# Indirect writes of routed rows placed step by step, and block 2's rows loaded and transposed later, in a recurrence-plus-experts kernel

## The chip, the cores and the metric

One core of one Trainium2 chip runs the whole kernel; the other cores are idle. The metric is device time in microseconds of one execution, lower is better. The kernel before took 364.48 us in the median of three runs (362.39, 364.92, 364.48).

The engines are called as in the profile: PE (TensorE, the matrix engine; its weight loads are PEld), DVE (VectorE), ACT (ScalarE), POOL (GpSimd) and SP (SyncE, which here only issues transfers). Each engine runs its own list of instructions in order and waits for the others on semaphores.

## The reference, cut to what matters

```python
# r, k, v, w: (4, 8, 768, 48); u: (8, 48)
for t in range(S):                       # a recurrence over 768 steps for each batch and head
    cur = u * k_t (outer) v_t
    y[:, :, t] = r_t @ (state + cur)
    state = w_t * state + k_t (outer) v_t
x = y.transpose(0, 2, 1, 3).reshape(3072, 384)
logits = x @ w_gate + modality_bias[modality_id]       # 8 experts
e_idx = argmax(logits); gate_w = softmax(logits)[e_idx]
for e in range(8):                       # each row goes through one expert only
    out[rows of e] = gate_w * (relu(x @ w1[e]) @ w2[e])   # 384 -> 1024 -> 384
```

## The kernel before

**Two stages.** The first stage (the scan, `att_iter`) goes through 24 units of 128 rows, one iteration `i` of a software pipeline each, and leaves each unit's 128 x 384 result (with its gate weight and row id, 386 columns) in SBUF. The second stage runs the experts over blocks of rows sorted by expert: blocks 0 and 1 have 512 rows, blocks 2 to 4 have 384, block 5 has 512 and block 6 has 416. A block is gathered by a plain load from the DRAM tensor `xs`, in which each row has been put at its sorted place.

**How rows get to their place.** Unit n is written by one indirect DMA on POOL's queue (`scatter(n)`, L692), 128 rows of 1544 bytes; the row numbers stand in column n of `posT`. They come from a count on PE into the PSUM tile `pR` (`route_b`) and one DVE reduction of all units of a part (L573 and L574). Part 0 is units 0 to 9, ranked during the scan; part 1 is units 10 to 23, ranked at the beginning of block 0's second half. `drain(n)` (L858) issues the next n writes that are due. The table `DRAIN` (L64) says after which scan iteration how many are issued: one each after iterations 15 to 20, and four after iteration 21. `LOAD` (L67) says after which iteration blocks 0 and 1 are loaded: 20 and 22. A load of `xs` waits for all writes issued before it, and a write behind a load waits until the load has read. Part 1's 14 writes are issued two at each of the steps 2 to 8 of block 0's down phase (L934).

**A block.** `blk_t` (L723) transposes a block's rows on PE into four PSUM pieces; ACT copies them rounded (`xh`), DVE takes the rest (`xo`). The up phase has 8 steps g of 9 matmuls (`blk_up`, L748), written alternately to two PSUM tiles pS0 and pS1; ACT makes `hh` of it and DVE `hl`, and only then is the PSUM tile free for step g + 2. The down phase goes through the block's groups j of 128 rows with 4 steps of 6 matmuls each (`blk_down`), step number 4j + g; each group is scaled by ACT (`ot`, L800) and written to `out` by an indirect DMA on POOL (L801). During these phases the weights are split into a rounded part and a rest for the next use: `w_split(1, ...)` (the second matrix, ACT cast L272 into `wh1`, DVE L273 into `wl1`) at the up steps 0, 2, 4 and 6, and `w_split(0, ...)` (the first one) in the down phase. For block 0 the first matrix is split at the scan's end with POOL doing the rests, three pieces in iteration 22 and five in iteration 23 (`split_some`, L326). The buffers `wh1` and `wl1` lie where the scan's tiles lay, part 0's rows among them, so their first cast waits until all ten writes of part 0 have read these rows.

**The order.** Everything is in program order, written by hand. What is interleaved with a block stands in a list by block, phase and step (`at(q, "u" or "d", step, ...)`), which `run` calls after that step's matmuls. `pad_rows` (L682) writes 128 zero rows behind each expert's rows, from SP's queue, at block 1's up steps 0 to 3, two each; SP issues them as soon as the counts are known. Block 2's load is issued at block 1's up step 4, and its `blk_t` stands between block 1's up and down phases:

```python
        for g in range(FC):
            blk_up(q, g)
            run(q, "u", g)
        if nxt is not None:
            blk_t(nxt)
        for j in range(nj):
            for g in range(FC // 2):
                blk_down(q, (2 * g, 2 * g + 1), (j,))
```

Of the kernel before, what the change touches and what calls it, by code (L numbers as in the profile page):

```python
# [14 lines left out]
ALU = mybir.AluOpType  # L15
AX = mybir.AxisListType

B, H, S, D = 4, 8, 768, 48
P = 128
NCH = S // P  # L20
NU = B * NCH
NT = B * S
DM = H * D
E, F = 8, 1024
KC = DM // P
FC = F // P
# [12 lines left out]
WB = NWA  # L39
# [15 lines left out]
PART = (10, 14)  # L55
FROM = (0, PART[0])
# [4 lines left out]
NEARLY = 3  # L61
SCATTER = PART[0] + 3
NEAR = 6
DRAIN = {**{SCATTER + 2 + n: 1 for n in range(NEAR)}, NU - 3: PART[0] - NEAR}  # L64
EARLY = 6
NPW = 3
LOAD = (SCATTER + 1 + NEAR, NU - 2)  # L67


@with_exitstack  # L70
def kernel(ctx: ExitStack, tc: tile.TileContext, rkw, vt, wf, cst, mid, wg, bias, w1, w2, out):
    nc = tc.nc
# [25 lines left out]
    def wt(n, tag, sh, bufs=None, dt=F32):  # L98
        T[tag, n] = (pa if tag in PREP else wk if tag in WORK else rt).tile(sh, dt, tag=tag, name=f"{tag}{n}", bufs=bufs)
        return T[tag, n]  # L100

    def pt(n, tag, sh=(P, 512)):
        T[tag, n] = (bp["s"] if tag in ("pS0", "pS1") else ps).tile(list(sh), F32, tag=tag, name=f"{tag}_{n}")
        return T[tag, n]
# [70 lines left out]
    posT = cp.tile([P, NU], I32, name="posT")  # L175
# [109 lines left out]
    def busy(i):  # L285
        return i in DRAIN and i < NU - 3

# [221 lines left out]
    units = lambda c: slice(FROM[c], FROM[c] + PART[c])  # L509
# [4 lines left out]
    def rcol(o, *sh):  # L514
        n = 1
        for d in sh:
            n *= d
        v = T["R"][:, o:o + n]
        return v if len(sh) == 1 else v.rearrange("p (a b) -> p a b", a=sh[0])

    C_RK, C_TAB = NU * E, 2 * NHX * E
# [34 lines left out]
    def route_b(c):  # L556

        n, oh = PART[c], T["oh", c]
        sh, ne = [P, n, E], NE(c)
        pR = T["R"][:, C_RK:C_RK + ne + 2 * E]  # L560

        def add(out, lhsT, rhs, start=False, stop=False):
            nc.tensor.matmul(out=out, lhsT=lhsT, rhs=rhs, start=start, stop=stop, skip_group_check=True)

        add(pR[:, 0:ne], trib, oh.rearrange("p a b -> p (a b)"), True)
        add(pR[:, 0:ne], onesb, ersb[:, None, :].to_broadcast(sh))
        if c:
            add(pR[:, 0:ne + E], onesb, ohs[:, None, :].to_broadcast([P, n + 1, E]))

        for j in range(n):  # L570
            m = n + (c == 0 and j < NEAR)
            add(pR[:, (j + 1) * E:(m + 1) * E], onesb, oh[:, j:j + 1].to_broadcast([P, m - j, E]), stop=j == n - 1)
        po, rk = posT[:, units(c)], rcol(C_RK, n, E)  # L573
        nc.vector.tensor_reduce(out=po, in_=rk, axis=AX.X, op=ALU.min)  # L574
        sm = wt(c, "sm", [P, NMOST, 1], 1)[:, 0:n]
        nc.vector.tensor_reduce(out=sm, in_=ex[:, 0:n], axis=AX.X, op=ALU.add)
        nc.vector.reciprocal(out=T["xp", c][:, :, DM:DM + 1], in_=sm)

    MAGIC = 12582912.0

# [105 lines left out]
    def rows_apart(key, ins):  # L686

        tc.declare_no_dep(ins.ins, group=key, reason="disjoint rows")
        tc.add_to_no_dep_group(key, ins.ins)

    def scatter(n):
        rows_apart("xs", nc.gpsimd.indirect_dma_start(out=xs[:, :], out_offset=bass.IndirectOffsetOnAxis(ap=posT[:, n:n + 1], axis=0),  # L692
                                     in_=T["xb", n], in_offset=None, bounds_check=XROWS - 1, oob_is_err=False))
# [12 lines left out]
    def width(q):  # L706
        return WIDTH[q] if isinstance(q, int) else BT

    def spans(w):
        return [(c, min(c + P, w)) for c in range(0, w, P)]  # L710

    def blk_load(q, at=None):
        at = q if at is None else at
        w = width(q) // P
        rest = width(q) % P
        xl = bp["m"].tile([P, BW // P, XW], F32, tag="xl", name=f"xl{q}", bufs=3)
        r = nc.sync.value_load(tab[0:1, 1, ds(at, 1)], min_val=0, max_val=DUMMY)
        nc.sync.dma_start(out=xl[:, 0:w], in_=xs[ds(r, w * P), :].rearrange("(j p) c -> p j c", p=P))
        if rest:
            nc.sync.dma_start(out=xl[0:rest, w], in_=xs[ds(r + w * P, rest), :])  # L720
        X["xl", q] = xl

    def blk_t(q):  # L723
        xl, w = X["xl", q], width(q)
        xh, xo = (bp["m"].tile([P, KC, BW], F32R, tag=t, name=f"{t}{q}", bufs=1) for t in ("xh", "xo"))
        pk, pu, nj = pt(f"x{q}_0", "pK", (P, 2, 512)), pt(f"x{q}_2", "pU"), w // P
        halves, m = [(0, KC - 1, (pk[:, 0], pk[:, 1])), (KC - 1, KC, (pu, pt(f"x{q}_3", "pX")))], w % P
        for c0, c1, pp in halves:
            for c in range(c0, c1):
                for j in range(nj):  # L730
                    for pb, r in zip(pp, HALVES):
                        o = ((c - c0) * nj + j) * 64
                        nc.tensor.transpose(out=pb[:, o:o + 64], in_=xl[r, j, c * P:(c + 1) * P], identity=ident[r, r])
        o = 64 * nj
        for c in range(KC if m else 0):
            nc.tensor.transpose(out=pu[:, o + c * m:o + (c + 1) * m], in_=xl[0:m, nj, c * P:(c + 1) * P], identity=ident[0:m, 0:m])
        view = lambda t, c0, c1, h: t[:, c0:c1, 0:nj * P].rearrange("p c (j h b) -> p c j h b", h=2, b=64)[:, :, :, h]
        moves = [(lambda t, c0=c0, c1=c1, h=h: view(t, c0, c1, h), pb[:, 0:(c1 - c0) * nj * 64].rearrange("p (c j b) -> p c j b", c=c1 - c0, j=nj))
                 for c0, c1, pp in halves for h, pb in enumerate(pp)]
        if m:  # L740
            moves.append((lambda t: t[:, :, nj * P:w], pu[:, o:o + KC * m].rearrange("p (c b) -> p c b", c=KC)))
        for at, pp in moves:
            nc.scalar.copy(out=at(xh), in_=pp)
        for at, pp in moves:
            nc.vector.tensor_tensor(out=at(xo), in0=pp, in1=at(xh).bitcast(F32), op=ALU.subtract)
        X["x", q] = (xh, xo)
# [109 lines left out]
    pend = []  # L856

    def drain(n):  # L858
        for _ in range(n):
            if pend:  # L860
                scatter(pend.pop(0))

    def hook_b(c):
        route_b(c)
# [2 lines left out]
    for i in range(-2, NU):  # L867
# [19 lines left out]

        drain(DRAIN.get(i, 0))
        if i in LOAD:
            blk_load(LOAD.index(i))  # L890
    assert not pend and not hooks
# [9 lines left out]
    seq = [*range(NQ)]  # L901
# [11 lines left out]
    def at(q, ph, step, *fn):  # L913
        aux.setdefault((q, ph, step), []).extend(fn)
# [5 lines left out]
    part = lambda fn, *a, **k: (lambda: fn(*a, **k))  # L920
    q0, q1 = seq[0:2]
# [8 lines left out]
    at(q0, "u", FC - 1, part(next, ra1), part(next, ra1), part(blk_raw, q1, 1))  # L930
    at(q0, "d", 0, part(route_x, 1))
    at(q0, "d", 1, part(hook_b, 1))
    for g in range(2, 4 * FC // 2):
        at(q0, "d", g, part(drain, 2))  # L934
        if g < 6:
            at(q0, "d", g, part(w_split, 0, g - 2))
        if 5 <= g < 8:
            at(q0, "d", g, part(more_table, 1, 2 - g // 7))
# [4 lines left out]
            at(q, "u", FC - 1, part(blk_raw, nq, 1))  # L943
    for e in range(E):
        at(q1, "u", e // 2, part(pad_rows, e))
    at(q1, "u", 4, part(blk_raw, seq[2], 0), part(blk_load, seq[2]))
    for k, q in enumerate(seq[1:1 + NG // 2]):
        for n, ph, step in ((2 * k, "u", 2), (2 * k + 1, "u", 6)):
            at(q, ph, step, part(guard_load, n))
# [11 lines left out]
    for n, q in enumerate(seq):  # L961
        nxt, nxt2 = (seq[n + d] if n + d < len(seq) else None for d in (1, 2))
        if nxt is None:
            bad, end, endh, rest = (nc.values_load(flg[0:1, i:i + 1], min_val=lo, max_val=hi)  # L964
                                    for i, lo, hi in ((0, 0, P), (1, NQ, HO), (2, HO, NTAB), (3, 0, P + NTAB)))
        nj = len(spans(width(q))) - (nxt is None)
        for g in range(FC):
            blk_up(q, g)
            run(q, "u", g)
        if nxt is not None:  # L970
            blk_t(nxt)
        for j in range(nj):
            for g in range(FC // 2):
                blk_down(q, (2 * g, 2 * g + 1), (j,))
                if nxt is not None and q != q0 and j == 0:
                    w_split(0, g)
                run(q, "d", (FC // 2) * j + g)
            if nxt2 is not None and q != q0:
                if j == 0:
                    blk_raw(nxt2, 0)  # L980
                if j == (2 if q == q1 else 0):
                    blk_load(nxt2)
            if q >= DRAIN_FROM and j == 0:
                nc.gpsimd.drain(fusable=False)  # L984
            if nxt is None and j == 1:
                strip_sum(q, nj)
                blk_out(q, (nj,))
            blk_out(q, (j,))
            if nxt is None and j == 0:
                strip_down(q, nj)  # L990
# [183 lines left out]
```

## Time and profile before

| what | value |
|---|---|
| median of three runs | 364.48 us (362.39 to 364.92) |
| the profiled execution, its own time | 362.38 us |
| its span (first to last instruction) | 360.6 us |
| mean granted PE clock over the span | 0.972 |
| PE busy | 338.0 us, 94% |
| DVE / ACT / POOL busy | 62% / 57% / 43% |
| end of the scan, first expert matmul | 129.4 us |
| block 1's up phase | 166.7 to 195.0 us |

The page shows one profiled execution. Times are us from the span's start. "Idle before" is what an engine waited ahead of an instruction and what ended that wait; "issue" means that nothing in the profile shows what the engine waited for, "remote" likewise for a semaphore whose sender is not seen. A granted clock of 1.00 is 2.4 GHz, 0.50 is 1.2 GHz. Matmul ends are modelled, so neighbouring rows of PE overlap; the distance of their starts is the pace.

### The profile page before, as it was taken

The page shows a single profiled execution, that of the slowest core. Times are in us where ns is not written, and L with a number is a line of the kernel's source. Part 1 is how long each engine was busy: PE and PEld are TensorE (multiplying, and loading weights), DVE is VectorE, ACT ScalarE, POOL GpSimd, SP SyncE. Part 2 cuts the span into 40 slices and gives each one's busy share as a digit, 9 for nine tenths or more (in the row PEclk, how much of TensorE's full clock was granted, in tenths as well). Part 3 has the DMA queues.
Part 4 walks back from the last instruction along what each step waited for, and adds up shares of the span by engine and source line. Part 5 has one row for each costly group of instructions (what it writes and reads, how often), then busy time and mean ns, then how long its engine had stood idle before and what let it go on. Part 6 is the DMA issues. An engine that isn't in the chain of part 4 may idle for free.

```text
span 360.6 us, 10329 instructions
## 1 busy us (share of the span) xinstructions
PE 338.0 (94%) x4064; PEld 306.5 (85%) x4064; DVE 224.4 (62%) x478; ACT 206.2 (57%) x524; POOL 155.1 (43%) x194
## 2 busy tenths in 40 slices
PE   8899999999989799997499999999999999999993
PEld 3688899989889687896278999999999988999973
DVE  6999999999997244880057936946526525814500
ACT  2576687878789373620046835956956934614320
POOL 5889999999982860077410220120120120121013
PEclk9999999999999789999589999999999999999998
DMA  7977887778864320036640430160260442210001
GB/s 229 399 242 227 287 291 267 248 258 259 284 225 135 97 82 0 3 139 249 217 164 3 148 137 2 29 236 0 51 236 2 153 158 89 88 58 29 1 25 56
DMA packets 18910, 52.30 MB, mean 145 GB/s; under 512 B 2405, under 2 KB 10405, under 8 KB 18852
## 3 DMA queue, kind: packets, MB, share of 16 engines
q1 hardware_dynamic: 15748, 42.08, 35.3%
q0 software_dynamic: 3104, 9.47, 7.0%
q8 instruction: 34, 0.56, 0.7%
q14 instruction: 24, 0.20, 0.2%
HBM read 55.43 MB, written 11.88 MB: 187 GB/s over the span
## 4 chain that ended last, share of the span: by engine, by line
issue 52%; PE 11%; POOL 9%; POOLq 2%; DMA 1%; ACT 0%; DVE 0%; ACTq 0%
POOL out L801 6%; PE pY L445 3%; POOL xs L692 2%; PE pS L401 2%; PE pY L434 1%; POOLq L984 1%; PE pR_x L317 1%; PE pR_x L494 1%; PE pU L419 1%; DMA xs<-xp,posT 1%; PE pS_u L756 1%; POOL wl L273 1%; POOLq L801 0%; POOLq L964 0%; POOL xp L549 0%
## 5 line engine op out<-in xcount | busy, mean ns | idle before, releaser
L801 POOL DMA_INDIRECT out<-ot,xl x25 | 26.0, 1039 | 157.8 <-ACT ot L800 156.6
L761 DVE SCALAR_TENSOR_TENSOR hl<-pS_u,hh 128x512 fp32r<-128x512 f32 (+2 forms) x56 | 34.6, 618 | 88.3 <-ACT hh L760 74.8
L756 PE MATMUL pS_u<-xh,wh 128*128 128x512 f32 (+2 forms) x168 | 63.1, 375 | 3.0 <-issue 3.0
L756 PE MATMUL pS_u<-xh,wl 128*128 128x512 f32 (+2 forms) x168 | 62.4, 371 | 2.4 <-issue 2.4
L760 ACT ACTIVATE hh<-pS_u 128x512 fp32r<-128x512 f32 (+2 forms) x56 | 30.3, 541 | 51.7 <-PE pS_u L756 50.3
L273 DVE TENSOR_TENSOR wl<-raw,wh 128x768 fp32r<-128x768 f32 x52 | 48.2, 954 | 3.1 <-ACT wh L272 2.6
L756 PE MATMUL pS_u<-xo,wh 128*128 128x512 f32 (+2 forms) x168 | 44.2, 369 | 1.7 <-issue 1.7
L272 ACT CAST wh<-raw 128x768 fp32r<-128x768 f32 (+1 forms) x60 | 45.1, 800 | 0.0
L756 PEld LDWEIGHTS pS_u<-xh,wh 128*128 128x128 f32 x168 | 32.1, 191 | 9.0 <-issue 5.9
L692 POOL DMA_INDIRECT xs<-xp,posT x24 | 24.9, 1040 | 32.3 <-issue 25.0
L777 PE MATMUL pY_d<-wh,hh 128*128 128x384 f32 x112 | 38.5, 344 | 0.0
L777 PE MATMUL pY_d<-wl,hh 128*128 128x384 f32 x112 | 37.6, 336 | 0.0
L777 PE MATMUL pY_d<-wh,hl 128*128 128x384 f32 x112 | 37.6, 336 | 0.0
L756 PEld LDWEIGHTS pS_u<-xh,wl 128*128 128x128 f32 x168 | 32.1, 191 | 5.8 <-issue 2.8
L756 PEld LDWEIGHTS pS_u<-xo,wh 128*128 128x128 f32 x168 | 31.3, 190 | 5.0 <-issue 1.6
L331 DVE TENSOR_TENSOR_SCAN pX_s<-pw,pX_s 128x268 f32<-128x268 f32 x48 | 34.1, 710 | 1.1 <-POOL pw L278 0.8
L283 POOL TENSOR_TENSOR G<-in 128x512 f32<-128x512 f32 x24 | 31.0, 1293 | 4.6 <-DMA in<-rkw 4.6
L445 PE MATMUL pY<-v,A 128*64 128x48 f32 x768 | 29.0, 225 | 2.9 <-issue 2.9
L342 ACT ACTIVATE dV<-v,dT 128x48 f32<-128x48 f32 x120 | 29.7, 325 | 0.1
L445 PEld LDWEIGHTS pY<-v,A 128*64 128x64 f32 x768 | 26.3, 141 | 4.0 <-issue 3.7
L403 DVE TENSOR_TENSOR A<-pS,cs 128x1024 f32<-128x1024 f32 x24 | 29.2, 1217 | 0.6 <-PE pS L401 0.6
L401 PE MATMUL pS<-R,K 64*128 64x128 f32 x384 | 26.9, 280 | 2.0 <-DVE A L403 1.2
(327 smaller groups left out, 679.9 us busy)
## 6 DMA issues: line engine op xcount, KB each, us to landing
raw<-w SPq DMA_DIRECT2D x24, 768.0 KB
in<-rkw SPq DMA_DIRECT2D x22, 768.0 KB
v<-vt SPq DMA_DIRECT2D x24, 192.0 KB
wg<-wf SPq DMA_DIRECT2D x8, 576.0 KB
raw<-w SPq DMA_DIRECT2D x8, 384.0 KB
xl<-xs SPq DMA_DIRECT2D x3, 772.0 KB
xl<-xs SPq DMA_DIRECT2D x4, 579.0 KB
xs<-zt SPq DMA_DIRECT2D x8, 193.0 KB
```

The costliest lines, as they stand in the source:

```text
L272: nc.scalar.copy(out=wh[k][:, sl], in_=raw[k][:, sl])
L273: (eng or (nc.vector, nc.gpsimd)[k]).tensor_tensor(out=wl[k][:, sl], in0=raw[k][:, sl], in1=wh[k][:, sl].bitcast(F32), op=ALU.subtract)
L283: nc.gpsimd.tensor_tensor(out=G, in0=t[:, 0:512], in1=t[:, 512:1024], op=ALU.mult)
L331: nc.vector.tensor_tensor_scan(out=BE[:, ::step], data0=pp[:, ::step], data1=d1[:, ::step], initial=0.0, op0=ALU.mult, op1=ALU.max)
L401: nc.tensor.matmul(out=pS[:, hh, p], lhsT=K[q, p], rhs=R[q, p], start=True, stop=True)
L445: nc.tensor.matmul(out=pY[q:q + 64, h * D:(h + 1) * D], lhsT=A[:, hh, p, q:q + 64], rhs=v[:, h * D:(h + 1) * D], start=(first(z) and h == ...
L692: rows_apart("xs", nc.gpsimd.indirect_dma_start(out=xs[:, :], out_offset=bass.IndirectOffsetOnAxis(ap=posT[:, n:n + 1], axis=0), in_=T["xb ...
L756: nc.tensor.matmul(out=pp, lhsT=wsrc[0][:, g, c * P:(c + 1) * P], rhs=xsrc[:, c, 0:w], start=(n == 0), stop=(n == 3 * KC - 1))
L760: nc.scalar.activation(out=hh, in_=pp, func=AF.Relu)
L761: nc.vector.scalar_tensor_tensor(out=hl, in0=pp, scalar=0.0, in1=hh.bitcast(F32), op0=ALU.max, op1=ALU.subtract)
L777: nc.tensor.matmul(out=X["y", q, j][0:r1 - r0], lhsT=hsrc[:, r0:r1], rhs=wsrc[1][:, f], start=(f == 0 and n == 0), stop=(f == FC - 1 and n ...
L801: ins = nc.gpsimd.indirect_dma_start(out=out[:, :], out_offset=bass.IndirectOffsetOnAxis(ap=xl[0:m, j, DM + 1:DM + 2].bitcast(I32), axis=0 ...
```

## The change

Three things. The 10 early writes: one each after iterations 15 to 22 and two after iteration 23, instead of one each to 20 and four after 21; block 1's load goes from iteration 22 to 23, behind the last of them. The 14 later writes: at block 0's down steps 2, 3, 4, 8 and 12, at block 1's eight up steps, and at its down step 0, one each; and the DVE reduction that makes a unit's row numbers is no longer made once for all 14 but one column at each write's step, just ahead of it in program order. Block 2: its load goes from block 1's up step 4 to its down step 1, its transposes from ahead of block 1's down phase to ahead of the last of its four groups; one of the PSUM pieces is then `pS1` in place of `pX`.

```diff
-DRAIN = {**{SCATTER + 2 + n: 1 for n in range(NEAR)}, NU - 3: PART[0] - NEAR}
+DRAIN = {**{SCATTER + 2 + n: 1 for n in range(PART[0] - 2)}, NU - 1: 2}
...
-LOAD = (SCATTER + 1 + NEAR, NU - 2)
+LOAD = (SCATTER + 1 + NEAR, NU - 1)
...
-        po, rk = posT[:, units(c)], rcol(C_RK, n, E)
-        nc.vector.tensor_reduce(out=po, in_=rk, axis=AX.X, op=ALU.min)
+        if c == 0:
+            place(0, n)
...
+    def place(n, k):
+        c = int(n >= PART[0])
+        nc.vector.tensor_reduce(out=posT[:, n:n + k], in_=rcol(C_RK + (n - FROM[c]) * E, k, E), axis=AX.X, op=ALU.min)
...
-        halves, m = [(0, KC - 1, (pk[:, 0], pk[:, 1])), (KC - 1, KC, (pu, pt(f"x{q}_3", "pX")))], w % P
+        halves, m = [(0, KC - 1, (pk[:, 0], pk[:, 1])), (KC - 1, KC, (pu, pt(f"x{q}_3", "pS1" if q == WB else "pX")))], w % P
...
-                scatter(pend.pop(0))
+                n = pend.pop(0)
+                if n >= PART[0]:
+                    place(n, 1)
+                scatter(n)
...
+    for q, ph, steps in ((q0, "d", (2, 3, 4, 8, 12)), (q1, "u", range(FC)), (q1, "d", (0,))):
+        for g in steps:
+            at(q, ph, g, part(drain, 1))
     for g in range(2, 4 * FC // 2):
-        at(q0, "d", g, part(drain, 2))
...
-    at(q1, "u", 4, part(blk_raw, seq[2], 0), part(blk_load, seq[2]))
+    at(q1, "u", 4, part(blk_raw, seq[2], 0))
+    at(q1, "d", 1, part(blk_load, seq[2]))
...
-        if nxt is not None:
+        if nxt is not None and q != q1:
             blk_t(nxt)
         for j in range(nj):
+            if q == q1 and j == nj - 1:
+                blk_t(nxt)
```

**Place 1, POOL at the scan's end.** xs<-xp is a write of one unit's rows, dV belongs to the scan, wl is the rest of block 0's first matrix, xp<-tidi fills in the row ids of part 1.

```order
 L354 TENSOR_TENSOR dV_2540<-v_2298,dT_2469 128x192
-L692 DMA xs<-xp_385,posT 29184x386 x4
-L354 TENSOR_TENSOR dV_2652<-v_2411,dT_2589 128x192
+L696 DMA xs<-xp_385,posT 29184x386
+L354 TENSOR_TENSOR dV_2643<-v_2411,dT_2589 128x192
 L273 TENSOR_TENSOR wl_69<-raw_66,wh_68 128x384 x3
-L354 TENSOR_TENSOR dV_2738<-v_2524,dT_2683 128x192
+L696 DMA xs<-xp_385,posT 29184x386
+L354 TENSOR_TENSOR dV_2721<-v_2524,dT_2674 128x192
 L273 TENSOR_TENSOR wl_69<-raw_66,wh_68 128x384 x5
+L696 DMA xs<-xp_385,posT 29184x386 x2
 L549 COPY xp_1423<-tidi 128x14
```

The four writes in a row become one, one and two; the last two now stand behind all eight rests of block 0's first matrix.

**ACT at block 0's first up steps**, the same in both kernels. wh_2864 is `wh1`; the names that begin with DMASW are the semaphores of POOL's writes.

```order
L760 ACTIVATE hh_0_2880<-pS_u_0_2870 128x512 [waits DMAHW3_49,DMAHW2_49,DMAHW5_49,PE_49,Activation_49]
L481 COPY xT_2886<-pX_('x', 0)_2885 128x384 [waits PE_49]
L272 CAST wh_2864<-raw_67 128x768 [waits DMASW4_49,DMASW3_49,DMASW5_49,DMASW2_49,DMASW6_49,DMASW1_49,DMASW7_49,DMASW0_49,DMAHW7_49,Activation_49,Pool_49]
L760 ACTIVATE hh_1_2903<-pS_u_1_2893 128x512 [waits PE_49]
L481 COPY xT_2908<-pX_('x', 1)_2907 128x384 [waits PE_49]
L760 ACTIVATE hh_2_2923<-pS_u_2_2913 128x512 [waits PE_49]
```

Nothing moved here; the cast waits for the writes of place 1, and the second up step's `hh_1` stands behind the cast.

**Place 2, POOL from block 0's down phase on.** Before:

```order
L692 DMA xs<-xp_1423,posT 29184x386 x4
L801 DMA out<-ot_0_3128,xl_2529 3072x384
L692 DMA xs<-xp_1423,posT 29184x386 x8
L801 DMA out<-ot_1_3216,xl_2529 3072x384
L692 DMA xs<-xp_1423,posT 29184x386 x2
L801 DMA out<-ot_2_3252,xl_2529 3072x384
L801 DMA out<-ot_3_3282,xl_2529 3072x384
L801 DMA out<-ot_0_3609,xl_2726 3072x384
```

And in the changed kernel, on the same engine:

```order
L696 DMA xs<-xp_1423,posT 29184x386 x2
L805 DMA out<-ot_0_3123,xl_2529 3072x384
L696 DMA xs<-xp_1423,posT 29184x386
L805 DMA out<-ot_1_3191,xl_2529 3072x384
L696 DMA xs<-xp_1423,posT 29184x386
L805 DMA out<-ot_2_3225,xl_2529 3072x384
L696 DMA xs<-xp_1423,posT 29184x386
L805 DMA out<-ot_3_3259,xl_2529 3072x384
L696 DMA xs<-xp_1423,posT 29184x386 x9
L805 DMA out<-ot_0_3591,xl_2821 3072x384
```

Nine of the 14 writes now stand behind block 0's last output write; each of the nine waits for its own DVE reduction, which stands behind that up step's `hl` on DVE.

**Place 3, PE around block 1's down phase** (xl_3465 and xl_3544 hold block 2's rows). Before, ahead of the first group:

```order
L756 MATMUL pS_u_7_3509<-xo_3029,wh_68 128x512 x3
L733 MATMUL pK_x_0_3527<-cs,xl_3465 128x64 x12
L733 MATMUL pU_x_2_3528<-cs,xl_3465 128x64
L733 MATMUL pX_x_3_3529<-cs,xl_3465 128x64
L733 MATMUL pU_x_2_3528<-cs,xl_3465 128x64
```

Now, between the third group and the fourth:

```order
L781 MATMUL pY_d_2_3656<-wh_2864,hl_7_3514 128x384
L737 MATMUL pK_x_0_3723<-cs,xl_3544 128x64 x12
L737 MATMUL pU_x_2_3724<-cs,xl_3544 128x64
L737 MATMUL pS_x_3_3725<-cs,xl_3544 128x64
L737 MATMUL pU_x_2_3724<-cs,xl_3544 128x64
```

The same 18 transposes moved behind three groups of the down phase.

## Rows read from the trace of the kernel before

**Rows 1.** Busy time of each engine, page part 1.
```profile
PE 338.0 (94%) x4064; PEld 306.5 (85%) x4064; DVE 224.4 (62%) x478; ACT 206.2 (57%) x524; POOL 155.1 (43%) x194
```

**Rows 2.** Stages: from:to, length, busy by engine (instructions), PE clock, DMA share, GB/s.
```profile
122.00:124.50 2.50, 1.74 (x22) 1.27 (x23) 0.00 (x0) 0.06 (x1) 2.48 (x4) 0.50 0.29 110
124.50:129.40 4.90, 4.90 (x90) 4.76 (x90) 2.50 (x5) 3.99 (x12) 2.30 (x4) 0.57 0.54 165
149.20:166.70 17.50, 17.50 (x119) 17.28 (x114) 11.49 (x42) 5.89 (x11) 9.91 (x9) 1.00 0.38 136
166.70:180.00 13.30, 6.39 (x18) 3.59 (x17) 0.00 (x0) 1.11 (x3) 7.86 (x8) 0.74 0.65 224
```

**Rows 3.** Waits, 166 to 183 us: us in total, times, longest.
```profile
ACT ot L800 <- remote: 19.7, 2, 10.1
...
PE pS_u L756 <- issue: 7.1, 9, 1.1
```

**Rows 4.** Timeline of PE, block 1's up phase: start, us, instruction.
```profile
166.73 0.39 PE L756 MATMUL pS_u<-xh,wh 128*128 128x512 f32 x1
...
179.60 1.48 PE L756 MATMUL pS_u<-xo,wh 128*128 128x512 f32 x3
181.32 0.80 PE L756 MATMUL pS_u<-xh,wh 128*128 128x512 f32 x1 [0.24 <-issue]
...
184.42 0.40 PE L756 MATMUL pS_u<-xh,wh 128*128 128x512 f32 x1
...
186.52 0.40 PE L756 MATMUL pS_u<-xh,wh 128*128 128x512 f32 x1
...
195.01 0.59 PE L733 MATMUL pK_x<-cs,xl 64*128 64x64 f32 x12
```

**Rows 5.** Timelines of POOL (two writes) and SP (zero rows), 154 to 172 us.
```profile
154.23 1.79 POOL L692 DMA_INDIRECT xs<-xp,posT  x1 [19.54 <-issue]
...
165.60 0.98 POOL L692 DMA_INDIRECT xs<-xp,posT  x1 [0.30 <-issue]
...
159.25 12.15 SPq L684 DMA_DIRECT2D xs<-zt  x6
```

**Rows 6.** The group of L692, first and last start; PE's longest wait, 84 to 112 us.
```profile
L692 POOL DMA_INDIRECT xs<-xp,posT x24: 968/982/1787, 85.2 to 174.6; - x24
...
PE pY L445 <- issue: 0.7, 1, 0.7
```

**Rows 7.** Timelines of POOL and SP, end of the scan.
```profile
109.08 0.99 POOL L692 DMA_INDIRECT xs<-xp,posT  x1 [0.15 <-issue]
...
117.59 1.00 POOL L692 DMA_INDIRECT xs<-xp,posT  x1 [6.98 <-DMA xl<-xs]
...
128.88 4.91 POOL L273 TENSOR_TENSOR wl<-raw,wh 128x384 fp32r<-128x384 f32 x5 [2.60 <-ACT wh L272]
...
111.98 12.88 SPq L718 DMA_DIRECT2D xl<-xs  x2
```

**Rows 8.** PE's waits, 118 to 124 us.
```profile
PE pY L445 <- issue: 1.6, 4, 0.5
...
PE pR_x L494 <- ACT dT L319: 0.7, 1, 0.7
```

**Rows 9.** Timelines of PE, ACT and DVE at block 0's up phase.
```profile
129.43 0.50 PE L756 MATMUL pS_u<-xh,wh 128*128 128x512 f32 x1
...
137.03 0.51 PE L756 MATMUL pS_u<-xh,wh 128*128 128x512 f32 x1
...
132.74 0.85 ACT L272 CAST wh<-raw 128x768 fp32r<-128x768 f32 x1
...
133.62 1.00 DVE L273 TENSOR_TENSOR wl<-raw,wh 128x768 fp32r<-128x768 f32 x1
134.90 0.69 DVE L761 SCALAR_TENSOR_TENSOR hl<-pS_u,hh 128x512 fp32r<-128x512 f32 x1 [0.28 <-ACT hh L760]
```

**Rows 10.** Timeline of DVE: the reduction that the change cuts up.
```profile
152.72 0.26 DVE L574 TENSOR_REDUCE posT<-pR_x 128x14 int32<-128x112 f32 x1
```

## The prediction

> **What bounds the kernel now.** I read the busy times first: PE is busy for 338.0 of 360.6 us [rows 1], so only time in which PE stands still or runs at the lower clock is to be had. The busy times by stage say where: in the whole second half PE has one hole, block 1's up phase [rows 2]. From 166.7 to 180.0 us it is busy for 6.39 of 13.3 us, at a mean granted clock of 0.74, beside a DMA share of 0.65. The timeline gives the size: from the first up matmul at 166.73 to the transposes at 195.01 are 28.3 us [rows 4]; eight undisturbed steps of 2.10 us (184.42 to 186.52, same rows) are 16.8. So 11.5 us are lost there.
>
> The waits say how. PE waits nine times for "issue", 7.1 us in all, and ACT waits for "remote" for 19.7 us ahead of two evictions [rows 3]. So no engine waits for data that another one is late with; instructions themselves come late, on PE, ACT and SP alike. SP needs 12.15 us for six plain writes of zero rows [rows 5], two us each. At that time POOL issues its indirect writes without a break, one in 1.28 us (0.98 of work and 0.30 of gap), from 154.23 on [rows 5] to the last at 174.6 [rows 6]. The same picture stands, smaller, at the scan's end: four writes in a row from 117.59 on [rows 7], and PE waits four times for "issue" and once for ACT, 2.3 us together [rows 8], then runs at a clock of 0.50 and 0.57, that is mostly at 1.2 GHz, until 129.4 [rows 2]. Against that, six single writes between 85.2 us [rows 6] and 109.08 [rows 7], some 4.8 us apart, leave PE with no wait for "issue" over 0.7 us [rows 6]. I read this as: indirect writes back to back hold up the delivery of instructions, single ones hardly do.
>
> **The early writes (place 1).** What goes: 2.3 us of waits [rows 8]. The low clock behind them covers 7.4 us in which PE is busy for 6.6 [rows 2]; at 2.4 GHz that work would be shorter by a third at most, since small matmuls don't double: 2.4 us. So the first expert matmul, now at 129.43, could come 4.7 us earlier, at 124.7, and the fourth up step, now at 137.03 [rows 9] and 7.6 us behind the first, at 132.3.
>
> What comes: a wait. The last two early writes now stand on POOL behind the five rests of 4.91 us, which begin at 128.88 and wait for ACT's casts [rows 7]. PE's earlier pace brings ACT's casts forward, but by less than 4.7 us, since ACT has its own work ahead of them; I take 3.1 us. Then the rests end at 130.7, the ninth write starts at 130.85 and the tenth at 132.15. How long a write needs to land: the sixth starts at 109.08 and the load that waits for it starts at 111.98 [rows 7], 2.9 us. So the tenth lands at 135.05. For that ACT's first cast into `wh1` waits, and behind the cast on ACT stands `hh_1`, behind the rest on DVE stands `hl_1`, and the fourth up step waits for `hl_1`'s PSUM tile. Cast 0.85, rest 1.00, `hl` 0.69 [rows 9], some 0.1 of semaphores: the fourth step starts at 137.7 instead of 137.03. Before it PE stands still for 5.4 us (132.3 to 137.7), and I expect the clock at 1.2 GHz for the next steps, as behind the hole of block 1. There the three matmuls from 179.60 take 1.72 us to the next start instead of 0.70, and the nine from 181.32 to 184.42 take 3.10 instead of 2.10 [rows 4], 2.0 us together. So the scan's end costs 0.7 + 2.0 = 2.7 us where four writes in a row cost nothing net.
>
> Bounds: if the cast doesn't wait, 4.7 us are won. If PE is no earlier at all, the writes start 3.1 us later, the fourth step comes at 140.8, and with the clock 5.8 us are lost. I take +2.7, since the wait is in the program and only the shift of 3.1 us is a guess.
>
> The Trainium skill ("DMA: Bandwidth & Descriptors", section "Anatomy of one DMA — SWDGE (gpsimd) path") fits such a write with 2.0 us and its bytes by 436 GB/s. That gives an estimate of 2.45 us for 128 rows of 1544 bytes, where the rows show 2.9 us to the waiting load. By the page the term would be 2.25 us instead of 2.7; the rows' figure is used.
>
> **The later writes (place 2).** In block 0's down phase 5 writes and 4 outputs are left where 11 indirect writes stood by 168 us, and the other nine come one to an up step, 2.1 us apart: the reduction ahead of each stands behind that step's `hl` on DVE, so POOL can't run ahead of PE. If PE is held up, the writes are held up with it. That excludes a loss at this place beyond today's 11.5 us, and bounds the gain by 0 and 11.5. A distance of 2.1 us lies between the bad 1.28 and the harmless 4.8, and the eight zero-row writes still run beside the first of them. I take 2.5 us as left over (a fifth of the hole, with its clock), so a gain of 9.0.
>
> The 14 small reductions replace one of 0.26 us [rows 10]; at no more than that each they are 3.6 us of DVE, spread over phases in which DVE is busy for 11.49 of 17.5 us or not at all [rows 2]. They cost nothing; without that cover, 3.6 us less the 0.26. What waits behind them is only the write itself.
>
> **Block 2 (place 3).** Let U be the end of block 1's up phase. The last write's reduction stands behind the last `hh`, `hl`, one cast and one rest, each under 1.0 us [rows 9]; the write starts at about U + 3, lands at U + 5.9, and only then can SP load 384 rows. Block 0's load of 512 rows, issued at 111.98, released POOL at 117.59 [rows 7]: 5.6 us. So block 2's rows are there by U + 11.5. The transposes now stand behind three groups of the down phase, 4.2 us each (17.5 us for a transpose and four [rows 2]): U + 12.5. The margin is 1 us and the term is 0; it costs what the load is late, up to 3 us by these rows. Copies and rests of the transposed rows have the last group's 4.2 us as cover. POOL's outputs, SP's load of block 3 and the weights' transfers keep their order behind them.
>
> **The sum.** +2.7 - 9.0 + 0 = -6.3 us on the profiled execution: span 360.6 to 354.3, its own time 362.38 to 356.1. The profiled execution is the fastest of three, the median lies 2.1 us above it. I take 1.2 us of that for a typical run: 357.3.
>
> **Rivals.**
> 1. *The cast's wait is harmless* because the writes land earlier or PE isn't there yet: then the early part gains 4.7 and all goes as hoped, 362.38 - 4.7 - 9.0 + 1.2 = 349.9 us. For it: the skipped hole at the scan's end. Against: the cast waits in the program for all of POOL's semaphores. Chance 0.12.
> 2. *Zero rows and writes crowd as before.* Six zero-row writes in 12.15 us [rows 5] are as many bytes as six units, they stay where they are, and the hole only begins when they run. If they, more than the distance, make it, half the hole stays: 362.38 + 2.7 - 5.7 + 1.2 = 360.6. Chance 0.18.
> 3. *Slower: the new wait at its full price, and nothing for it.* If the late instructions have another cause than the writes' distance, PE isn't earlier at the scan's end (+5.8) and the hole stays (0): 362.38 + 5.8 + 1.2 = 369.4 us. It decides from the point where the early part costs more than block 1 gives back. For it: single instructions 1.4 us apart don't look like a transfer that waits its turn. Against: both holes lie on the writes, and none elsewhere. The Trainium skill ("Runtime: NRT & Kernel Launch", section "Instruction fetch mechanics") speaks for this rival: engines fetch instructions ahead in large blocks over a queue of their own, mostly hidden. By that rule writes shouldn't starve an engine that runs straight on; that ACT, PE and SP wait for nothing else at the same time [rows 3, 5] speaks against it here. Chance 0.17.
>
> **How the numbers follow.** My forecast has 0.53, with its own range of 353.5 to 361 (residue of the hole 0 to 5 us, early part 1 to 4). A measurement of this kernel can tell about 1% from no change, here 3.6 us: faster means below 360.8. Forecast: 0.48 faster, 0.05 within; rival 1: 0.12 faster; rival 2, at the edge: 0.07 faster, 0.11 within; rival 3: 0.03 within, 0.14 slower. Sums 0.67, 0.19, 0.14. The range of 350 to 366 leaves out most of rival 3 and half of rival 1.
>
> **What would show it.** Right: no row of PE with "issue" around block 1's up phase beyond about 2 us, that phase near 19 us, ACT's evictions of block 0 without "remote"; no gaps of PE around 120 us; the last two early writes behind POOL's fifth rest, ACT's first `wh1` cast waiting for a DMA, PE idle for some 5 us ahead of the fourth up step and a clock of 0.50 behind it. Wrong: PE's 1.4 us pace again in block 1; a fourth up step before 134 us; PE waiting for block 2's rows ahead of the fourth group.

## The result, and the profile after

| | kernel before | changed kernel |
|---|---|---|
| median of six runs each | 363.79 us (362.39 to 366.73) | 353.72 us (351.76 to 354.12) |
| ratio | | 0.972 (95% interval 0.968 to 0.976) |
| span of the profiled execution | 360.6 us | 352.2 us |

The change is faster by 2.8%, as forecast in kind; 357.3 us was predicted. Further down this turns out to hold on some chips only. A few executions of the kernels below ran in a slower state; ratios and their intervals leave these out, medians don't.

Page part 1 of the changed kernel, for [rows 1]:

```profile
PE 332.4 (94%) x4064; PEld 304.0 (86%) x4064; DVE 225.3 (64%) x491; ACT 206.0 (59%) x524; POOL 156.2 (44%) x194
```

Stages, for [rows 2], and two more around the fourth up step (length, busy by engine, PE clock, DMA share, GB/s):

```profile
122.00:124.50 2.50, 2.50 (x73) 2.38 (x70) 1.25 (x3) 2.48 (x9) 2.35 (x3) 1.00 0.03 7
124.50:129.40 4.90, 4.90 (x25) 3.99 (x26) 1.86 (x5) 3.18 (x8) 4.87 (x6) 1.00 0.11 40
129.40:137.00 7.60, 2.63 (x22) 1.86 (x21) 0.88 (x2) 1.74 (x4) 3.26 (x5) 0.90 0.24 66
137.00:142.00 5.00, 4.26 (x11) 2.94 (x13) 2.17 (x4) 1.19 (x3) 0.00 (x0) 0.50 0.37 137
149.20:166.70 17.50, 17.50 (x130) 16.63 (x129) 13.45 (x48) 8.41 (x15) 6.06 (x7) 1.00 0.24 89
166.70:180.00 13.30, 13.30 (x64) 11.24 (x63) 4.88 (x10) 4.41 (x7) 6.98 (x7) 1.00 0.80 260
```

From 166.7 to 180.0 us PE is now busy throughout, at a clock of 1.00, beside a DMA share of 0.80; before it was half idle beside 0.65. So the DMA engines' load alone was not what held it up. The stretch up to 129.4 us is clean as well. A new hole stands between 129.4 and 137.0, and behind it a clock of 0.50, that is 1.2 GHz.

PE's waits from 118 to 140 us, for [rows 8], all of them:

```profile
PE pS_u L760 <- DVE hl L765: 5.7, 1, 5.7
```

Timelines of the changed kernel around that wait (POOL, ACT, PE), for [rows 7, 9]:

```profile
125.56 4.89 POOL L273 TENSOR_TENSOR wl<-raw,wh 128x384 fp32r<-128x384 f32 x5
130.62 1.01 POOL L696 DMA_INDIRECT xs<-xp,posT  x1 [0.16 <-issue]
131.93 0.98 POOL L696 DMA_INDIRECT xs<-xp,posT  x1 [0.30 <-issue]
...
135.26 0.83 ACT L272 CAST wh<-raw 128x768 fp32r<-128x768 f32 x1 [7.48 <-issue]
...
124.36 0.49 PE L760 MATMUL pS_u<-xh,wh 128*128 128x512 f32 x1
...
137.74 0.80 PE L760 MATMUL pS_u<-xh,wh 128*128 128x512 f32 x1 [5.71 <-DVE hl L765]
```

The first expert matmul comes 5.1 us earlier (129.43 before), the fourth up step 0.7 later (137.03). ACT's first cast into `wh1` starts at 135.26, 3.3 us after the tenth write was issued; the profile calls that wait "issue", the program says it is for POOL's writes.

Timelines of block 1 (PE, POOL, SP), for [rows 4, 5]:

```profile
151.14 0.71 PE L737 MATMUL pK_x<-cs,xl 64*128 64x64 f32 x16
...
169.49 0.39 PE L760 MATMUL pS_u<-xh,wh 128*128 128x512 f32 x1
...
186.28 0.33 PE L781 MATMUL pY_d<-wh,hh 128*128 128x384 f32 x1
...
198.85 0.59 PE L737 MATMUL pK_x<-cs,xl 64*128 64x64 f32 x12
...
173.45 1.49 POOL L696 DMA_INDIRECT xs<-xp,posT  x1 [1.93 <-DVE posT L581]
175.55 0.98 POOL L696 DMA_INDIRECT xs<-xp,posT  x1 [0.61 <-DVE posT L581]
...
162.44 7.19 SPq L688 DMA_DIRECT2D xs<-zt  x6
...
193.32 0.39 SPq L722 DMA_DIRECT2D xl<-xs  x1
```

The up phase is 186.28 - 169.49 = 16.8 us long, exactly eight steps of 2.10. POOL waits for each step's reduction and writes every 2.1 us. SP's six zero-row writes take 7.19 us instead of 12.15. Block 2's rows are asked for at 193.32, and its transposes follow at 198.85 without a wait.

Where the 8.4 us of span went, by starts in PE's two timelines: block 0's up phase ends, at the transposes of block 1, 2.8 us later (148.37 before, 151.14 after). From block 1's first up matmul to block 2's it is 34.3 us instead of 45.7 (169.49 to 203.83; 166.73 to 212.47 before). +2.8 - 11.4 = -8.6.

### The profile page after: what moved, and what is told of

Same layout as the page of the kernel before. It is cut to its first block, busy times and chain, and to the rows that moved or that the text cites. A ratio compares the mean times of both kernels' runs of the same rounds, so it can differ in the third digit from the quotient of the medians.

```text
span 352.2 us, 10351 instructions
## 1 busy us (share of the span) xinstructions
PE 332.4 (94%) x4064; PEld 304.0 (86%) x4064; DVE 225.3 (64%) x491; ACT 206.0 (59%) x524; POOL 156.2 (44%) x194
## 4 chain that ended last, share of the span: by engine, by line
issue 42%; PE 39%; POOL 7%; ACT 2%; POOLq 2%; DVE 2%; ACTq 0%; DVEq 0%
PE pS_u L760 8%; PE pS L401 5%; PE pY L445 5%; POOL out L805 5%; PE pR_x L317 3%; PE pY L434 3%; PE pY_d L781 2%; PE pU L419 2%; PE pX_d L781 2%; PE pR_x L494 2%; POOLq L996 1%; POOL wl L273 1%; POOL xs L696 1%; DVE wl L273 1%; ACT dV L342 0%
## 5 line engine op out<-in xcount | busy, mean ns | idle before, releaser
L696 POOL DMA_INDIRECT xs<-xp,posT x24 | 27.1, 1129 | 42.0 <-DVE posT L581 33.8
L295 POOL TENSOR_TENSOR in<-in 128x512 f32<-128x512 f32 (+1 forms) x23 | 28.3, 1230 | 0.6
L445 PE MATMUL pY<-v,A 128*64 128x48 f32 x768 | 26.9, 222 | 1.0 <-issue 1.0
```

The source lines that it names most:

```text
L445: nc.tensor.matmul(out=pY[q:q + 64, h * D:(h + 1) * D], lhsT=A[:, hh, p, q:q + 64], rhs=v[:, h * D:(h + 1) * D], start=(first(z) and h == ...
```

## The experiments

The experiments ran on several chips of the same kind, with runs of the kernel before beside them on each. The chips turned out to matter, so each is given a letter. "Block 0" and "block 1" are the lengths of these blocks' up phases, from the first up matmul to what PE does behind them, by PE's timeline of each profile.

| run | chip | kernel before, us | this, us | ratio, 95% interval | block 0 | block 1 |
|---|---|---|---|---|---|---|
| kernel before (profile above) | | 363.79 | | | 18.9 | 28.3 |
| changed kernel (profile above) | | 363.79 | 353.72 | 0.968 to 0.976 | 26.8 | 16.8 |
| later_alone | A | 363.34 | 350.20 | 0.960 to 0.968 | 18.9 | 16.8 |
| one_reduction | A | 363.34 | 360.75 | 0.983 to 0.996 | 26.4 | 22.6 |
| crowd_pads_late | A | 363.34 | 370.15 | 1.017 to 1.027 | 18.9 | 28.9 |
| early_2_2 | A | 363.34 | 348.18 | 0.956 to 0.963 | 20.4 | 16.8 |
| dense_128 | B | 348.50 | 361.60 | 1.031 to 1.053 | 25.8 | 16.8 |
| dense_16 | B | 348.50 | 361.63 | 1.032 to 1.052 | 28.6 | 16.8 |
| block2_early | B | 348.50 | 366.98 | 1.045 to 1.070 | 28.3 | 16.8 and 9.7 idle |
| early_2_2_cast | B | 348.50 | 345.37 | 0.987 to 0.995 | 18.9 | 16.8 |
| after_again | C | 349.30 | 354.08 | 1.011 to 1.028 | 26.3 | 16.8 |
| dense_128_again | C | 349.30 | 360.90 | 1.027 to 1.052 | 26.4 | 16.8 |
| before_again | D | 346.58 | 351.46 | 0.990 to 1.033 | 18.9 | 16.9 |
| both_mended | E | 363.69 | 348.13 | 0.951 to 0.960 | 18.9 | 16.8 |

**The later part alone (later_alone).**

```diff
-DRAIN = {**{SCATTER + 2 + n: 1 for n in range(PART[0] - 2)}, NU - 1: 2}
+DRAIN = {**{SCATTER + 2 + n: 1 for n in range(NEAR)}, NU - 3: PART[0] - NEAR}
-LOAD = (SCATTER + 1 + NEAR, NU - 1)
+LOAD = (SCATTER + 1 + NEAR, NU - 2)
```

> The change without its early part: the ten early writes and block 1's load stand as in the kernel before, the later writes and block 2 as in the changed one. Theory (the early part costs 2.8 us, the later part gains 11.3): the early part's cost goes, 353.7 - 2.8 = 350.9 us, with block 1's up phase free of holes and some 17 us long, and the gaps around 120 us and the clock of 0.50 behind them back. Rival (the early part is needed or harmless, the whole gain comes of both together): 353.7 us or more.

350.20 us, 3.5 below the changed kernel on a chip with the same hole, though four early writes in a row bring back PE's waits for "issue" (six, 2.4 us in all) and the lower clock (0.67 from 124.5 to 129.4 us). The early part of the change costs, and the later part wins more without it.

**One reduction for all units (one_reduction).**

```diff
-        if c == 0:
-            place(0, n)
+        place(FROM[c], n)
...
-                n = pend.pop(0)
-                if n >= PART[0]:
-                    place(n, 1)
-                scatter(n)
+                scatter(pend.pop(0))
```

> The changed kernel, but the row numbers of all 14 later units come from one DVE reduction as before, so POOL's writes wait for no step's work and run ahead of PE; the order of POOL's list is unchanged. Theory (writes back to back hold up the instructions, the distance is what helps): after block 0's last output, near 171 us, nine writes follow one another in 1.28 us each, the hole comes back in block 1's up phase, 5 to 11 us of it: 359 to 365 us, with PE waiting for 'issue'. Rival (the five writes fewer in block 0's down phase, or block 2's later load, were what helped; distance doesn't matter): 353.7 us within 1.

POOL's order is the same, only nothing holds it back. The timelines of POOL, ACT and PE:

```profile
172.44 0.98 POOL L695 DMA_INDIRECT xs<-xp,posT  x1 [0.30 <-issue]
173.72 0.98 POOL L695 DMA_INDIRECT xs<-xp,posT  x1 [0.30 <-issue]
...
182.73 0.98 POOL L695 DMA_INDIRECT xs<-xp,posT  x1 [0.30 <-issue]
...
181.12 0.60 ACT L763 ACTIVATE hh<-pS_u 128x512 fp32r<-128x512 f32 x1 [3.21 <-PE pS_u L759]
185.43 0.60 ACT L763 ACTIVATE hh<-pS_u 128x512 fp32r<-128x512 f32 x1 [3.71 <-PE pS_u L759]
...
177.79 0.86 PE L759 MATMUL pS_u<-xo,wh 128*128 128x512 f32 x3
...
179.89 0.86 PE L759 MATMUL pS_u<-xo,wh 128*128 128x512 f32 x3
182.50 0.50 PE L759 MATMUL pS_u<-xh,wh 128*128 128x512 f32 x1 [1.75 <-issue]
...
186.80 0.50 PE L759 MATMUL pS_u<-xh,wh 128*128 128x512 f32 x1 [1.94 <-DVE hl L764]
```

Nine writes stand in a row, and 5.8 us of the hole are back (22.6 instead of 16.8). The engine that is late is ACT: its eviction `hh` of the fourth step starts 2.5 us after the last matmul that it reads (177.79 + 0.86), that of the fifth 4.7 us after (179.89 + 0.86), with the engine idle before either. PE waits for the PSUM tiles behind them, ahead of 182.50 and 186.80, and then runs at a mean clock of 0.58 for a step. So on chip A it is not enough to put the writes at later steps in the program; the reductions that tie each write to its step are worth 5.8 us in this phase, and some 7 us of the time (360.75 against 353.72 on a chip with the same hole). The other half of the hole stays away without them. Whether the five writes fewer in block 0's down phase or block 2's later load keep it away was not separated.

**Zero rows held back, writes crowded as before (crowd_pads_late).** Besides the early part and the reduction of the kernel before:

```diff
-    for q, ph, steps in ((q0, "d", (2, 3, 4, 8, 12)), (q1, "u", range(FC)), (q1, "d", (0,))):
-        for g in steps:
-            at(q, ph, g, part(drain, 1))
     for g in range(2, 4 * FC // 2):
+        at(q0, "d", g, part(drain, 2))
...
+    at(q1, "u", FC - 1, part(nc.vector.memset, zt[:, 0:DM], 0.0))
     for e in range(E):
-        at(q1, "u", e // 2, part(pad_rows, e))
+        at(q1, "d", 0, part(pad_rows, e))
```

> The kernel before with block 2's load and transposes late as in the changed one, and the zero-row writes held back until block 1's up phase is over (the buffer of zeros is zeroed once more by DVE at the last up step). The early part, the one reduction and the two writes to a step are those of the kernel before. Theory (indirect writes back to back make the hole alone): the hole stays, 10 to 12 us of it, 362 to 365 us. Rival (the zero-row writes of SP, crowding with them, make it): the hole goes, about 364 - 11 = 353 us; half of it each would give 358.

Its stage and its waits from 163 to 196 us:

```profile
166.70:180.00 13.30, 5.33 (x21) 3.49 (x19) 0.00 (x0) 0.54 (x2) 8.03 (x9) 0.83 0.53 179
```

```profile
DVE hl L764 <- ACT hh L763: 25.3, 6, 18.2
ACT ot L803 <- remote: 15.1, 1, 15.1
...
PE pS_u L759 <- DVE hl L764: 7.8, 1, 7.8
...
PE pS_u L759 <- issue: 1.5, 3, 0.9
```

The hole is whole (28.9 us) with no zero row on its way, so rival 2 of the prediction falls on this chip. Here ACT stands still for 15.1 us ahead of an eviction whose matmuls are long done, and PE runs out of PSUM tiles behind it. The total is above the expected 362 to 365: the zero rows, held back, make block 2's load late, PE waits 4.7 us for it, and its mean clock is 0.76 behind (213 to 220 us).

**Another early part (early_2_2), and the casts a step later (early_2_2_cast).**

```diff
-DRAIN = {**{SCATTER + 2 + n: 1 for n in range(PART[0] - 2)}, NU - 1: 2}
+DRAIN = {**{SCATTER + 2 + n: 1 for n in range(NEAR)}, NU - 3: 2, NU - 2: 2}
-LOAD = (SCATTER + 1 + NEAR, NU - 1)
+LOAD = (SCATTER + 1 + NEAR, NU - 2)
...
-        at(q0, "u", 2 * g, part(w_split, 1, g, eng=vec))
+        at(q0, "u", 2 * g + 1, part(w_split, 1, g, eng=vec))
```

The last two lines are in early_2_2_cast alone.

> The changed kernel with another early part: single writes after iterations 15 to 20, two after 21 and two after 22, none after 23, block 1's load after 22. The last two then stand ahead of the five rests on POOL, not behind them. Theory (the fourth up step waits 5.7 us for the tenth write's landing and then runs at 1.2 GHz for 2 us more): the tenth starts near 125.6, lands near 128.5, ACT's first cast into wh1 waits under 1 us, the fourth step starts near 132 and the clock stays at 2.4 GHz: 353.7 - 5.7 - 2.0 = 346 us, up to 348. Rival (pairs of writes already hold up the instructions as four in a row do): gaps around 118 to 126 us and a low clock, 350 to 352 us.

348.18 us, just above the expected 346 to 348. The tenth write starts at 125.91, ahead of POOL's five rests, and the fourth step at 133.73 instead of near 132, after a wait of 1.3 us; beside the pairs of writes PE's timeline shows no wait for "issue".

```profile
125.91 0.97 POOL L696 DMA_INDIRECT xs<-xp,posT  x1 [0.30 <-issue]
...
133.73 0.51 PE L760 MATMUL pS_u<-xh,wh 128*128 128x512 f32 x1 [1.34 <-DVE hl L765]
```

> The kernel with pairs of early writes after iterations 21 and 22 (348.2 us), and block 0's casts into wh1 one step later (up steps 1, 3, 5, 7 instead of 0, 2, 4, 6). Theory (what is left of the wait, 1.3 us ahead of the fourth up step, is ACT's first cast waiting for the tenth write): it goes, 346.9 us. Rival (the last cast and rest are late for the down phase, or something else sets the fourth step): 348.2 us or more.

345.37 us, on a chip where the kernel before takes 348.50. Block 0's up phase is 18.9 us long instead of 20.4: the wait is gone. The two totals come from different chips, so their difference is not the casts' worth.

**More writes to a step (dense_128, dense_16).** Each up step of block 1 writes its unit once more, to rows of `xs` that no block reads; in dense_16 only 16 of the 128 rows.

```diff
+        ap = apart[0:m, n:n + 1] if far else posT[0:m, n:n + 1]
...
                 scatter(n)
+                if PART[0] + 5 <= n < NU - 1:
+                    scatter(n, P, True)
```

> The changed kernel with one more indirect write behind each of the eight writes of block 1's up phase: the same 128 rows once more, to rows of xs that no block reads. Two writes to a step of 2.1 us are more than POOL can issue (1.29 us each), so it issues without a break for some 20 us, though each step's pair still waits for that step. Theory (writes without a break hold up the instructions): the up phase, 16.8 us without a hole, takes 21 to 27 us; block 2's rows come some 4 us later and PE may wait for them: 358 to 367 us. Rival (running ahead of the steps, not the writes' distance, made the hole): the up phase stays within 1 us of 16.8, 353.7 to 358 us for block 2's rows alone.

> As the run with one more full write to each step, but the additional writes have 16 rows instead of 128. Theory 'issuing' (the work of preparing an indirect write on POOL holds up the other engines): the up phase is about as long as with full writes. Theory 'traffic' (the rows on their way do): with an eighth of the additional rows the up phase stays within 1 us of 16.8, and the time is 353.7 to 357 us.

POOL issues without a break from 172.7 to 200.7 us (173.7 to 201.4 with short ones), and block 1's up phase stays at 16.8 us. But on this chip the kernel before takes 348.50 us, 15 us less than on chip A, so this says nothing yet about a chip with a hole. The extra 7 us or so are block 2's: from the end of block 1's up phase to block 2's first up matmul dense_128 takes 25.1 us instead of 17.6, with a wait of 4.8 us ahead of the transposes and a mean clock of 0.62 behind it (203 to 211 us).

```profile
202.95 0.80 PE L738 MATMUL pK_x<-cs,xl 64*128 64x64 f32 x10 [4.77 <-DMA xl<-xs]
```

**Block 2's transposes at their old place (block2_early).**

```diff
-    for q, ph, steps in ((q0, "d", (2, 3, 4, 8, 12)), (q1, "u", range(FC)), (q1, "d", (0,))):
+    for q, ph, steps in ((q0, "d", (2, 3, 4, 8, 12)), (q1, "u", (*range(FC), FC - 1))):
...
-    at(q1, "d", 1, part(blk_load, seq[2]))
+    at(q1, "u", FC - 1, part(blk_load, seq[2]))
...
-        if nxt is not None and q != q1:
+        if nxt is not None:
             blk_t(nxt)
...
-            if q == q1 and j == nj - 1:
-                blk_t(nxt)
```

> The changed kernel without its last part: block 2's transposes stand ahead of block 1's down phase again, its load at block 1's last up step, ahead of it the last two writes (the ninth of these moves from the down phase's first step to the last up step). Theory (the later place is what makes room for the writes): the last write starts about 2 us after the up phase, lands 2.9 us later, the load takes 4 to 5.6 us: PE waits 8 to 10 us ahead of the transposes, and some steps behind run at 1.2 GHz: 353.7 + 9 + 1.5 = 364 us, the whole gain gone. Rival (the transfers are faster than these rows, or the place doesn't matter): 354 to 357 us.

366.98 us, above the expected 364. PE waits 9.7 us ahead of the transposes, as expected, and runs at a mean clock of 0.88 behind:

```profile
197.51 0.91 PE L737 MATMUL pK_x<-cs,xl 64*128 64x64 f32 x12 [9.74 <-DMA xl<-xs]
```

```profile
197.50:210.00 12.50, 12.49 (x78) 12.38 (x79) 9.87 (x40) 10.13 (x18) 0.98 (x1) 0.88 0.29 85
```

Writes spread over the up phase like this are affordable only because the transposes moved with them.

**The same kernels on other chips (after_again, dense_128_again, before_again).** No edit; before_again is the kernel before itself, so its ratio of 0.990 to 1.033 only shows how far its runs scatter there.

> The changed kernel as it is. In the call before, on another chip, the kernel before took 348.5 us instead of 363. Theory (the hole in block 1's up phase belongs to that first chip, and the later part of the change gains nothing where there is no hole): where the kernel before takes some 363 us, the changed one takes 353 to 354; where it takes some 348.5, the changed one takes 349 to 354, slower or the same, by the early part's 2.8 us and no gain behind it. Rival (the changed kernel is faster by 11 us there too): 338 to 341 us.

> The same kernel as the run with one more full write to each step, once more, since its 361.6 us were taken on a chip where the kernel before shows no hole's time: there its up phase was 16.8 us long and PE waited 4.8 us for block 2's rows. Theory (writes without a break hold up the instructions, on chips of the first kind): where the kernel before takes some 363 us the up phase is 20 to 27 us long, 362 to 370 us in all; where it takes some 348.5, the up phase stays at 16.8 us. Rival (only POOL running ahead of the steps makes the hole): 16.8 us on either.

> The kernel before as it is, for its profile on another chip. Theory (the late instructions belong to some chips and not to others): where it takes some 348 to 350 us, block 1's up phase shows 16.8 us without a wait for 'issue', though POOL issues its 14 writes and four outputs without a break as on the first chip, and ACT's evictions of block 0 show no 'remote'; the four early writes in a row still cost some of the 2.3 us at the scan's end or nothing. Where it takes some 363 us, the hole of 11.5 us is there again. Rival (the 14 us come from somewhere else, the scan or the later blocks): the hole is there at 349 us too.

On chip C the changed kernel takes 354.08 us as ever, the kernel before 349.30: the change is slower there, by 1.1 to 2.8%. On chip D the kernel before left its profile. First the page's busy line, then the scan's end and a stage of block 1's up phase as long as that of [rows 2], then POOL's timeline:

```profile
PE 330.7 (95%) x4064; PEld 303.2 (87%) x4064; DVE 225.7 (65%) x478; ACT 206.2 (59%) x524; POOL 155.9 (45%) x194
```

```profile
124.50:129.40 4.90, 4.09 (x69) 3.67 (x70) 2.42 (x5) 4.13 (x13) 4.90 (x7) 1.00 0.58 181
164.70:178.00 13.30, 13.30 (x59) 10.70 (x58) 6.33 (x8) 6.26 (x10) 9.63 (x9) 1.00 0.81 228
```

```profile
152.18 1.79 POOL L692 DMA_INDIRECT xs<-xp,posT  x1 [18.45 <-issue]
...
163.57 0.98 POOL L692 DMA_INDIRECT xs<-xp,posT  x1 [0.30 <-issue]
164.85 0.98 POOL L692 DMA_INDIRECT xs<-xp,posT  x1 [0.30 <-issue]
...
175.93 0.98 POOL L801 DMA_INDIRECT out<-ot,xl  x1 [0.30 <-issue]
```

It is the same program, the same crowd of writes, most of them 1.29 us apart, from 152.18 to the last output at 175.93, and zero rows beside them, yet PE is busy for 13.30 of 13.30 us where [rows 2] have 6.39. The hole is not in the program alone. dense_128_again fell on chip C and so, like its first run, left untested whether writes tied to their steps but without a break make a hole on a chip like A.

**The mended kernel on one more chip (both_mended).** The kernel of early_2_2_cast, unchanged.

> The kernel with pairs of early writes and the later casts (345.4 us beside 348.5 for the kernel before on one chip) once more, on whichever chip it falls. Theory (the later part removes the hole where there is one and costs nothing where there is none; the mended early part removes the wait): 344 to 347 us either way, that is 16 to 18 us faster than the kernel before where that takes some 363 us, and 2 to 5 us faster where it takes some 348. Rival (on a chip with the hole, pairs and single writes still cost some of it): 348 us or more beside 363.

348.13 us beside 363.69, above the expected 344 to 347 and at the rival's number. Both up phases have their undisturbed length (18.9 and 16.8), so nothing is left of the hole there. The profiled run, the slowest of six (346.44 to 350.43), is later already at the first expert matmul, 127.72 against 123.64 on chip B. Most of that comes between 82 and 109 us, where the six single writes stand: by POOL's timeline the run is 1.1 us behind that of chip B at the beginning and 3.6 at the end, and POOL waits three times for the scan's input loads meanwhile (1.57, 0.44 and 1.12 us; once for 0.59 on chip B). What makes these loads late is not shown, so the rival's reason, that single writes still cost something on a chip with the hole, stays open for the scan. This version beats the kernel before on either sort of chip: by 4.4% (4.0 to 4.9) where the hole is, by 0.9% (0.5 to 1.3) where it isn't. Beside the changed kernel it never ran, but the changed kernel's ratios are higher on both sorts (0.972 and 1.020).

## Why the prediction was right, and where it was wrong

**The early part (+2.7 us): right, step by step.** The first up matmul was put at 124.7 and came at 124.36; the tenth write at 132.15, came at 131.93; the fourth step at 137.7, came at 137.74. The clock behind was 0.50 for the nine matmuls from 137.74 on, which take 4.79 us to the next step's first instead of some 2.8 (139.78 - 137.03, the same step before). +2.8 measured. Two inputs were lucky: the shift of POOL's rests, a guess of 3.1 us, was 3.3 (128.88 to 125.56), and the 2.0 us for the clock were read from rows in which 0.24 us are a wait for "issue". later_alone confirms the sign, and early_2_2 the place: with the tenth write ahead of the rests 4.4 of the 5.7 us are gone.

**The later writes (-9.0 us): right in kind, too small.** The step that was off is "I take 2.5 us as left over". Nothing is left: 16.8 us, and 11.4 us gained with what stands behind. Writes 2.1 us apart, each tied to its step, made no hole on any chip here; whether the distance or the tie does it on a chip with the hole was not tested.

**Block 2 (0 us): right.** The load was put at U + 5.9 and went out at U + 7.0 (U is 186.28), the transposes at U + 12.6 without a wait. Two misses offset each other: the load went out 1.1 us late, but such a load takes 4.0 to 4.5 us (block2_early, from 193.46 to 197.51; dense_128, from 198.48 to 202.95) where 5.6 were taken from a larger one. What it would cost if late is shown by dense_128 (4.8 us of wait) and block2_early (9.7 us).

**The reductions (0 us): right.** 0.16 us each, in DVE's shadow.

**The addition of 1.2 us for a typical run** was not needed: the profiled execution of the changed kernel took 353.98 us, the median is 353.72. With the 2.4 us above, this is the whole distance from 357.3.

**The reading behind it: incomplete.** "I read this as: indirect writes back to back hold up the delivery of instructions" is right for chip A, where rival 2 fell and the hole came back with the crowd. It is not right in general: on chips B, C and D the kernel before took 346.6 to 351.5 us in the medians, and the profile from D shows the crowd and no hole. The prediction took one profile of one chip for the program's own behaviour. There rival 3's condition holds, in a milder form: no hole to lose, so nothing to gain, and the early part's cost remains. The loss on chip C, 1.1 to 2.8% or 4 to 10 us, takes in that rival's +5.8, and the profiles show its reason: without late instructions the scan's end is hardly brought forward (first expert matmul at 127.39 in the kernel before on D, 126.65 in the changed one on C), and the new wait stands at nearly its full price (block 0's up phase 18.9 and 26.3 us). Block 1's first up matmul comes 6.6 us later (164.68 and 171.24), and from there to block 2's both take 34.35 us.

**What stays open** is what the late instructions are. In the kernel before, PE, ACT and SP were slowed at once, without data to wait for, and in one_reduction ACT was late while PE's steps still followed one another in 2.10 us. In the kernel before, the transfers from 166 to 182 us, by queue, are these:

```profile
q0 software_dynamic: 648, 2.01, 32.5%
q1 hardware_dynamic: 733, 1.40, 28.4%
```

The queues that the profile calls "instruction" move one packet each between 150 and 166 us and none in the hole, and the DMA share is lower there than in the same stretch of the undisturbed runs (0.65 against 0.80 and 0.81). So, as far as the profile shows, it is neither a shortage of transfer time nor a block of instructions on its way. The Trainium skill ("Runtime: NRT & Kernel Launch", section "Instruction fetch mechanics") has instructions fetched ahead in blocks, mostly out of sight; the silent queues agree with that, and it does not explain the late instructions. Whether it is the chip itself, the time at which it was used (each letter stands for one occasion), or where the program and its tensors were put on it can't be told from these runs.

## What to carry to other kernels

A wait for "issue" or "remote" on several engines at once, with no data late, may belong to the chip on which the profile was taken: take the kernel before on a second chip before removing it. If it must be removed, tie each indirect write to the step it stands at by a small operation that it depends on, since a later place in the program alone lets POOL run ahead (5.8 us here). And before moving a write, look for who waits until all of them have landed: here a cast two engines away cost more than the gaps that the move removed.

## What the runs showed that was not expected

- The same program takes 362 to 367 us on some chips and 345 to 355 on others, with nearly the whole difference that the profiles show (13.3 us of span) in two places: block 1's up phase (28.3 against 16.9 us) and the granted clock at the scan's end (0.57 from 124.5 to 129.4 us [rows 2], 1.00 in the same stretch on chip D).
- An indirect write of 16 rows occupies POOL for 0.88 us, one of 128 rows for 1.00 (medians of dense_16's group): POOL's time hardly depends on the rows.
